# The first MoE's weights decoded in pairs of 768 columns, in place in four staging buffers

## The chip, the cores and the metric

The kernel runs on one core of one Trainium2 chip. Its time is the device time of one execution in microseconds (us); the figure for a kernel is the median over its runs. All work of the reference is done in this one launch.

## The reference

A recurrent attention with a decaying state feeds a gated MoE layer, and that feeds a second layer with SoLU and LayerNorm. 3072 tokens (4 sequences of 768) of 384 features pass through all three.

```python
# attention: r, k, v, w of shape (4, 8, 768, 48), u of (8, 48)
for t in range(S):
    cur = einsum('bhd,bhe->bhde', u[None] * kt, vt)
    y[:, :, t] = einsum('bhd,bhde->bhe', rt, state + cur)
    state = wt[:, :, :, None] * state + einsum('bhd,bhe->bhde', kt, vt)
# first MoE: w_gate, w_val (384, 1536), w_out (1536, 384)
g = x @ w_gate
x = (g / (1 + exp(-g)) * (x @ w_val)) @ w_out
# second MoE: w_in (384, 1024), w_out (1024, 384)
h = x @ w_in
solu = h * softmax(h)
out = layernorm(solu) * g_ln @ w_out
```

The weights of both MoE layers come as 64-bit floats. The kernel makes 32-bit floats of them on the chip ("decoding") and then splits each into a high part in the format fp32r and the low rest; a product is made of three matmuls (high by high, high by low, low by high).

## The kernel before

**Order.** The program first collects every operation with an engine, an assumed duration, a priority and its dependencies in a `Graph`; `emit` then plays these through a list scheduler and writes the instructions of each engine in that order. So each engine runs a fixed sequence, and a priority or an assumed duration changes where an instruction stands. A DMA is a resource of that plan like an engine; all DMAs are issued by one queue, that of SP, in the planned order, and an issue waits there until its target buffer is free.

**Blocks.** The 3072 tokens go in six groups `q` of 512 (128 of each sequence). Of the first group the first MoE runs its first six hidden tiles `m` (of 128 columns; 12 in all) on two halves of 256 tokens, one after the other, and then the other six on all 512; the groups `q` from 1 on run all 12 at 512. One such step is a unit (`moe1_unit`): nine matmuls for the gate projection (PSUM tile `ps` or `psa` from `xh`, `xl` and `hg`, `lg`; `h` and `l` for high and low), nine for the value projection (`hv`, `lv`), SiLU on ScalarE into `sg`, the product on VectorE in `sg`, its split into `mh` (copy on ScalarE) and `ml` (subtraction on VectorE), and, after the next unit's projections, nine matmuls with `ho`, `lo` that add to three PSUM banks. The attention's tiles (24, by group and sequence: `feat`, `tok`, `vv` are loaded, VectorE scans and scales) are spread between the units of the group ahead.

**Weights.** In the first group, with the first half and then with the full-width units, `weight` loads and decodes gate, value and output weights of `m`, 384 columns of 128 rows each (393 KB as 64-bit floats), at a priority 1.8 units ahead of the unit that uses them. The load goes to one of three staging tiles `st`, shifted by one byte, so that the words of the tile can be used as they lie. `decode8` then takes, for each weight:

- ScalarE copies the top bytes of the numbers to `tb` (L331 `tb<-st`, 384 bytes per row);
- VectorE's L378 and L381 rearrange bits in `tb`, 96 words each, with the start of `dc` as scratch;
- ScalarE's L384 writes `tb`, scaled, to the 384 words of `dc`;
- VectorE's L386 shifts the low word from `st` and joins it with `dc`; after it `st` is free;
- ScalarE copies `dc` to the high part (`hg`, `hv` or `ho`);
- VectorE subtracts (L328 `lg`, `lv` or `lo`); after it `dc` is free. For `m` 0 this low part is made by two matmuls into PSUM (L453, L454) and a copy on ScalarE instead.

There are two `dc` and two `tb`. Behind the first group's last unit no weight is left to decode, and the `st` tiles serve as buffers for results that go to DRAM.

**Fills.** As long as the planner finds nothing for TensorE before its time 80, it puts in matmuls of the identity (L1157). There are 81 of them in the program, 46 ahead of the first projection; each leaves two matmul records in the trace (162).

Of the kernel before, what the change touches and what calls it, by code (L numbers as in the profile page):

```python
# [38 lines left out]
NEX = 4  # L39
NFLAT = 8  # L40
# [194 lines left out]
def attn_moe_moe2_kernel(  # L235
# [88 lines left out]
    def words(src):  # L324
        return src.bitcast(U32) if wide else src
# [19 lines left out]
    def t_act(n):  # L345
        return 0.1 + n / 1200
# [15 lines left out]
    def decode(prio, st, dc, n, skey, dkey):  # L362
        if not wide:
            return st[:, 0:n], skey
        s3 = st[:, 0:2 * n].rearrange("p (n t) -> p n t", t=2)
        a = dc[:, 0:n]

        for z in range(3):
            g.add("DVE", 0.07 + (0.2 if z == 0 else 0.4) * n / DM, prio, lambda z=z: decode_op(z, s3, a), [skey], [dkey],
                  port=True)  # L370
        return a.bitcast(F32), dkey

    def decode8(prio, st, dc, t8, skey, dkey, tkey):
        tops = st.bitcast(I8)[:, 8:8 * DM + 8:8]
        b, a = t8.bitcast(I8), dc.bitcast(I32)
        n4 = DM // 4
        g.add("ACT", t_act(DM), prio, copy(b, tops), [skey], [tkey])
        g.add("DVE", 0.17, prio, lambda: DVE.tensor_scalar(out=dc[:, 0:n4], in0=t8, scalar1=0x07070707, scalar2=3,  # L378
                                                           op0=ALU.bitwise_and, op1=ALU.logical_shift_left),
              [tkey], [dkey], port=True)  # L380
        g.add("DVE", 0.17, prio, lambda: DVE.scalar_tensor_tensor(  # L381
            out=t8, in0=t8, scalar=0xC0C0C0C0, in1=dc[:, 0:n4], op0=ALU.bitwise_and, op1=ALU.bitwise_or),
              [dkey], [tkey], port=True)
        g.add("ACT", t_act(DM), prio, lambda: ACT.activation(out=a, in_=b, func=AF.Copy, scale=float(1 << 24)),  # L384
              [tkey], [dkey])
        g.add("DVE", 0.47, prio, lambda: DVE.scalar_tensor_tensor(  # L386
            out=dc, in0=st[:, 1:2 * DM:2], scalar=5, in1=dc, op0=ALU.logical_shift_right, op1=ALU.bitwise_or),
              [skey], [dkey], port=True)
        return dc.bitcast(F32), dkey
# [35 lines left out]
    def weight(w, m, prio):  # L425
        i = nst[0]
        nst[0] += 1
        st, dc = ST[i % 3], DC[i % 2]
        sk, dk = ("st", i % 3), ("dc", i % 2)
        ws, sd = words(W1[w]), st[:, 0:DM * sz]  # L430
        z = sz
        if wide:
            ws, sd, z = W1[w].bitcast(U8), st.bitcast(U8)[:, 1:8 * DM + 1], 8
        if w == "o":
            fn = dma(sd, ws[m * 128:(m + 1) * 128, :])
        else:
            fn = dma(sd.rearrange("p (k f) -> p k f", k=KD),
                     ws[:, m * 128 * z:(m + 1) * 128 * z].rearrange("(k p) f -> p k f", p=128))
        first = g.dma(0.55 * sz, prio - 10, fn, [], [sk])
        if wide:  # L440
            a, ak = decode8(prio, st, dc, TB8[i % 2], sk, dk, ("tb8", i % 2))
        else:
# [794 lines left out]
```

## Time and profile before

| | before |
|---|---|
| time, median of 3 runs | 765.27 us |
| lowest and highest | 764.41 and 766.58 us |
| span of the profiled execution | 766.4 us |
| TensorE (PE) busy | 754.6 us, 98% |
| VectorE (DVE) busy | 574.3 us, 75% |
| ScalarE (ACT) busy | 333.7 us, 44% |
| GpSimd (POOL) busy | 60.8 us, 8% |
| chain that ended last | PE 85%, DVE 6%, DMA 4%, ACT 2% |

The profile is one execution with a span of its own, 766.4 us, from its first instruction to its last; the total time of that execution is not listed apart. Busy time counts recorded instructions, overlapping ones once; the recorded time of a VectorE or ScalarE instruction is longer than the step to the next one's start, since the next starts before the last has fully drained. The chain is followed back from the last instruction, at each step to what it waited for. [...]

### The profile page before, as it was taken

The page shows a single profiled execution, that of the slowest core. Times are in us where ns is not written, and L with a number is a line of the kernel's source. Part 1 is how long each engine was busy: PE and PEld are TensorE (multiplying, and loading weights), DVE is VectorE, ACT ScalarE, POOL GpSimd, SP SyncE. Part 2 cuts the span into 40 slices and gives each one's busy share as a digit, 9 for nine tenths or more (in the row PEclk, how much of TensorE's full clock was granted, in tenths as well). Part 3 has the DMA queues.
Part 4 walks back from the last instruction along what each step waited for, and adds up shares of the span by engine and source line. Part 5 has one row for each costly group of instructions (what it writes and reads, how often), then busy time and mean ns, then how long its engine had stood idle before and what let it go on. Part 6 is the DMA issues. An engine that isn't in the chain of part 4 may idle for free.

```text
span 766.4 us, 16301 instructions
## 1 busy us (share of the span) xinstructions
PE 754.6 (98%) x6393; PEld 649.7 (85%) x6393; DVE 574.3 (75%) x1286; ACT 333.7 (44%) x747; POOL 60.8 (8%) x53
## 2 busy tenths in 40 slices
PE   8999999899999999999999999999999999999998
PEld 7899987688888888888888888888888988889998
DVE  8798998987776678667776643486788989899930
ACT  4777766353242334333334322333454442654541
POOL 0000000000000000000000000000011221623330
PEclk9999999999999999999999999999999999999999
DMA  7677575323333323323322210343331124234321
GB/s 216 178 232 234 164 233 162 113 71 89 97 104 103 98 78 94 113 78 86 96 82 88 77 40 14 117 130 114 95 124 62 54 75 114 79 100 108 92 86 47
DMA packets 60077, 83.09 MB, mean 108 GB/s; under 512 B 18272, under 2 KB 43360, under 8 KB 60000
## 3 DMA queue, kind: packets, MB, share of 16 engines
q1 hardware_dynamic: 60000, 82.05, 36.8%
q8 instruction: 50, 0.82, 0.5%
q14 instruction: 27, 0.22, 0.1%
HBM read 60.25 MB, written 10.22 MB: 92 GB/s over the span
## 4 chain that ended last, share of the span: by engine, by line
PE 85%; DVE 6%; DMA 4%; ACT 2%; SPq 1%; issue 1%; ACTq 0%; DVEq 0%
PE ps L753 15%; PE ps L754 14%; PE ps L755 14%; PE pb L1135 4%; PE pb L1136 4%; PE pb L1137 4%; PE hp L1027 4%; PE hp L1028 4%; PE hp L1029 3%; PE psa L753 3%; PE psa L755 3%; PE psa L754 3%; PE ps L1157 2%; DMA st<-w_out 2%; SPq L1120 1%; DMA st<-w_val 1%
## 5 line engine op out<-in xcount | busy, mean ns | idle before, releaser
L754 PE MATMUL ps<-ml,ho 128*128 128x512 f32 (+1 forms) x234 | 87.6, 374 | 1.2 <-DVE ml L328 1.1
L753 PE MATMUL ps<-mh,ho 128*128 128x512 f32 (+1 forms) x234 | 88.0, 376 | 0.3 <-ACT mh L331 0.3
L755 PE MATMUL ps<-mh,lo 128*128 128x512 f32 (+1 forms) x234 | 87.2, 373 | 0.0
L331 ACT ACTIVATE mh<-sg 128x512 fp32r<-128x512 f32 (+1 forms) x78 | 46.4, 596 | 87.6 <-DVE sg L328 87.1
L788 ACT ACTIVATE sg<-ps 128x512 f32<-128x512 f32 (+1 forms) x57 | 32.9, 577 | 86.9 <-PE ps L755 86.1
L328 DVE TENSOR_TENSOR ml<-sg,mh 128x512 fp32r<-128x512 f32 (+1 forms) x78 | 50.2, 645 | 26.8 <-ACT mh L331 26.6
L753 PE MATMUL ps<-xh,hg 128*128 128x512 f32 (+1 forms) x171 | 67.5, 395 | 0.3 <-DVE xl L328 0.3
L328 POOL TENSOR_TENSOR xl<-x2s,xh 128x512 fp32r<-128x512 f32 x15 | 19.7, 1330 | 601.0 <-ACT xh L331 601.0
L754 PE MATMUL ps<-xl,hg 128*128 128x512 f32 (+1 forms) x171 | 65.8, 385 | 0.0
L755 PE MATMUL ps<-xh,lg 128*128 128x512 f32 (+1 forms) x171 | 65.7, 384 | 0.0
L1135 PE MATMUL pb<-o2h,th 128*128 128x384 f32 x192 | 65.0, 338 | 0.6 <-ACT ob L331 0.6
L1137 PE MATMUL pb<-o2h,tl 128*128 128x384 f32 x192 | 64.5, 336 | 0.0
L1136 PE MATMUL pb<-o2l,th 128*128 128x384 f32 x192 | 64.5, 336 | 0.0
L328 DVE TENSOR_TENSOR sg<-sg,ps 128x512 f32<-128x512 f32 (+1 forms) x53 | 34.1, 643 | 40.0 <-PE ps L755 39.0
L753 PE MATMUL ps<-xh,hv 128*128 128x512 f32 (+1 forms) x159 | 59.6, 375 | 0.5 <-ACT sg L788 0.5
L755 PE MATMUL ps<-xh,lv 128*128 128x512 f32 (+1 forms) x159 | 59.4, 373 | 0.0
L754 PE MATMUL ps<-xl,hv 128*128 128x512 f32 (+1 forms) x159 | 59.3, 373 | 0.0
L1027 PE MATMUL hp<-i2h,xh 128*128 128x512 f32 x144 | 57.0, 396 | 0.5 <-DVE sv L1044 0.5
L1028 PE MATMUL hp<-i2l,xh 128*128 128x512 f32 x144 | 56.6, 393 | 0.0
L1029 PE MATMUL hp<-i2h,xl 128*128 128x512 f32 x144 | 56.1, 390 | 0.0
L331 ACT ACTIVATE kt<-PR 32x256 f32<-32x256 f32 (+1 forms) x128 | 46.2, 361 | 22.6 <-DVE PR L605 21.2
L754 PEld LDWEIGHTS ps<-ml,ho 128*128 128x128 f32 x234 | 44.1, 188 | 9.6 <-DVE ml L328 1.9
(184 smaller groups left out, 1901.7 us busy)
## 6 DMA issues: line engine op xcount, KB each, us to landing
tok<-tok SPq DMA_DIRECT2D x20, 576.0 KB, 3.9
feat<-feat SPq DMA_DIRECT2D x24, 448.0 KB, 4.7
xt<-tb SPq DMA_DIRECT2D x128, 64.0 KB, 2.0
feat<-feat SPq DMA_DIRECT2D x24, 231.4 KB, 2.8
vv<-vv SPq DMA_DIRECT2D x24, 192.0 KB, 4.1
st<-w_gate SPq DMA_DIRECT2D x12, 384.0 KB, 4.0
st<-w_val SPq DMA_DIRECT2D x12, 384.0 KB, 4.0
st<-w_out SPq DMA_DIRECT2D x12, 384.0 KB, 4.3
```

Of the source, the lines that this page charges most:

```text
L328: return lambda: eng.tensor_tensor(out=out, in0=in0, in1=in1, op=op)
L331: return lambda: ACT.activation(out=out, in_=in_, func=AF.Copy)
L753: PE.matmul(out=o, lhsT=wh, rhs=xhi, start=first, stop=False)
L754: PE.matmul(out=o, lhsT=wh, rhs=xlo, start=False, stop=False)
L755: PE.matmul(out=o, lhsT=wl, rhs=xhi, start=False, stop=last)
L788: lambda: ACT.activation(out=sg, in_=pg.t[:, 0:n], func=AF.Silu), [pg.key], [sk]))
L1027: PE.matmul(out=hp()[:, f], lhsT=xh_[:, k, s], rhs=R["i2h"][:, k, f], start=(k == 0), stop=False)
L1028: PE.matmul(out=hp()[:, f], lhsT=xh_[:, k, s], rhs=R["i2l"][:, k, f], start=False, stop=False)
L1029: PE.matmul(out=hp()[:, f], lhsT=xl_[:, k, s], rhs=R["i2h"][:, k, f], start=False, stop=(k == KD - 1))
L1135: PE.matmul(out=po(), lhsT=th[:, m], rhs=R["o2h"][:, m], start=(m == 0), stop=False)
L1136: PE.matmul(out=po(), lhsT=th[:, m], rhs=R["o2l"][:, m], start=False, stop=False)
L1137: PE.matmul(out=po(), lhsT=tl[:, m], rhs=R["o2h"][:, m], start=False, stop=(m == M2 - 1))
```

## The change

Weights are decoded two at a time. A pair (`duos`) is gate and value of one `m`, or the output weights of two neighbouring `m`; the order is (gate, value) of `m`, (output of `m`, output of `m`+1), (gate, value) of `m`+1, and so on for even `m`: 18 pairs in place of 36 weights. Two loads fill the halves of one staging tile, of which there are now four (`NST`), each with room for 768 numbers. Each decoding step is one instruction for both: L367 and L370 of 192 words, and L373, L375, the copy to the high part and the subtraction of 768. The tile `dc` is gone: L367 uses the even words of the staging tile as scratch, L373 writes there, L375 joins them with the odd words in place, and copy and subtraction read the odd words, 8 bytes apart. The staging tile is thus free after the subtraction. The high and low parts of a pair are one tile each, named after its first (`hg`, `lg` hold gate and value). With `m` 0 the pairs (gate, value) of 0 and (output of 0, output of 1) take the low part through PSUM, one split per half. [...] Branches for weights that are not 64-bit go.

```diff
+NST = 4
-    WH = {(w, m): w1p.tile([128, KD, 128], F32R, name=f"h{w}{m}") for m in range(M1) for w in "gvo"}
-    WL = {(w, m): w1p.tile([128, KD, 128], F32R, name=f"l{w}{m}") for m in range(M1) for w in "gvo"}
-    ST = slots(stp, "st", [128, DM * sz + 2], 3, RAW)
-    DC = slots(stp, "dc", [128, DM], 2, U32)
-    TB8 = slots(stp, "tb8", [128, DM // 4], 2, U32)
+    duos = [d for m in range(0, M1, 2) for d in ((("g", m), ("v", m)), (("o", m), ("o", m + 1)), (("g", m + 1), ("v", m + 1)))]
+    WD = {d: [w1p.tile([128, 2, KD, 128], F32R, name=f"{x}{d[0][0]}{d[0][1]}") for x in "hl"] for d in duos}
+    WH, WL = ({y: WD[d][z][:, i] for d in duos for i, y in enumerate(d)} for z in range(2))
+    sz, RAW, N2 = 2, U32, 2 * DM
+    ST = slots(stp, "st", [128, 2 * N2 + 2], NST, RAW)
+    TB8 = slots(stp, "tb8", [128, N2 // 4], 2, U32)
...
+    def decode8(prio, st, t8, skeys, okey, ekey, tkey):
+        tops = st.bitcast(I8)[:, 8:8 * N2 + 8:8]
+        odd, even = st[:, 1:2 * N2:2], st[:, 2:2 * N2 + 2:2]
+        b, n4 = t8.bitcast(I8), N2 // 4
+        g.add("ACT", t_act(N2), prio, copy(b, tops), skeys, [tkey])
+        g.add("DVE", 0.07 + n4 / 960, prio, lambda: DVE.tensor_scalar(
+            out=even[:, 0:n4], in0=t8, scalar1=0x07070707, scalar2=3, op0=ALU.bitwise_and, op1=ALU.logical_shift_left),
+              [tkey], [ekey], port=True)
+        g.add("DVE", 0.07 + n4 / 960, prio, lambda: DVE.scalar_tensor_tensor(
+            out=t8, in0=t8, scalar=0xC0C0C0C0, in1=even[:, 0:n4], op0=ALU.bitwise_and, op1=ALU.bitwise_or),
+              [ekey], [tkey], port=True)
+        g.add("ACT", t_act(N2), prio, lambda: ACT.activation(
+            out=even.bitcast(I32), in_=b, func=AF.Copy, scale=float(1 << 24)), [tkey], [ekey])
+        g.add("DVE", t_dve(N2), prio, lambda: DVE.scalar_tensor_tensor(
+            out=odd, in0=odd, scalar=5, in1=even, op0=ALU.logical_shift_right, op1=ALU.bitwise_or),
+              skeys + [ekey], [okey], port=True)
+        return odd.bitcast(F32)
...
+    def weights(duo, prio):
+        i = nst[0] % NST
...
+        for z, (w, m) in enumerate(duo):
...
+            g.dma(1.1, prio - 10, fn, [], [sk[z]])
+        a = decode8(prio, st, t8, sk, ok, ek, tk)
+        h, l = (x.rearrange("p d k f -> p (d k f)") for x in WD[duo])
+        g.add("ACT", t_act(N2), prio, copy(h, a), sk + [ok], hk)
+        if duo[0][1] >= NLO:
+            g.add("DVE", t_dve(N2), prio, tt(DVE, l, a, h.bitcast(F32), ALU.subtract), sk + [ok] + hk, lk, port=True)
         else:
+            for z in range(2):
...
+                g.add("PE", 0.9, prio, fn, sk + [ok, hk[z], "ident", "nident"], take=[ps])
+                g.add("ACT", t_act(DM), prio, lambda ps=ps, c=c: copy(l[:, c], ps.t[:, 0:DM])(), [ps.key], [lk[z]])
...
             if c0 == 0 and q == 0:
-                for w in "gvo":
-                    weight(w, m, bstart[j] + UNIT[n] * (m - m0 - 1.8))
+                for d in duos:
+                    if d[0] == ("g", m) or d[0] == ("o", m):
+                        weights(d, bstart[j] + UNIT[n] * (m - m0 - 1.8))
...
-    nc = _bacc.Bacc("TRN2", target_bir_lowering=False, num_devices=1)
+    nc = _bacc.Bacc("TRN2", target_bir_lowering=False, num_devices=1, dynamic_dma_scratch_size=1024)
```

The new instructions stand at L367 (was L378), L370 (L381), L373 (L384), L375 (L386), L441 and L442 (L453 and L454); the fills are at L1144. Of the 81 fills before, 46 stand ahead of the first projection and 35 behind it; of the 60 now, 46 and 14.

The order changes at three places. The first is SP's queue at the start, from the third weight load of before on; `st` are the staging tiles (numbers tell tiles apart), `feat`, `vv`, `tok` and `u_tok` belong to the attention. Before:

L334 DMA st_178<-w_gate 128x3x1024
L334 DMA st_179<-w_val 128x3x1024
L334 DMA st_180<-w_out 128x3072
L334 DMA feat_207<-feat 112x529
L334 DMA u_tok<-u_rep 128x384
L334 DMA feat_206<-feat 112x1024
L334 DMA vv_208<-vv 128x384
L334 DMA tok_210<-tok 128x384
L334 DMA feat_207<-feat 112x1024
L334 DMA vv_209<-vv 128x384
L334 DMA tok_211<-tok 128x384
L334 DMA st_178<-w_gate 128x3x1024
```

Now:

L334 DMA st_142<-w_gate 128x3x1024
L334 DMA st_142<-w_val 128x3x1024
L334 DMA st_143<-w_out 128x3072
L334 DMA feat_170<-feat 112x529
L334 DMA st_143<-w_out 128x3072
L334 DMA st_144<-w_gate 128x3x1024
L334 DMA st_144<-w_val 128x3x1024
L334 DMA st_145<-w_gate 128x3x1024
L334 DMA st_145<-w_val 128x3x1024
L334 DMA u_tok<-u_rep 128x384
L334 DMA feat_169<-feat 112x1024
L334 DMA vv_171<-vv 128x384
```

Three weight loads stood ahead of the eight loads of the attention that are shown, and the fourth, which waits for its tile, behind them; now eight weight loads, into all four tiles, stand ahead of all but one of these.

The second is VectorE around the second unit, with decoding steps between the attention's products (`tok`, `AM`, `e`) and the unit's (`sg`, `ml`). Before:

L386 SCALAR_TENSOR_TENSOR dc_182<-st_178,dc_182 128x384
L486 SCALAR_TENSOR_TENSOR e_212<-feat_206,pat_f 112x528
L328 TENSOR_TENSOR ml_104<-sg_100,mh_102 128x256
L328 TENSOR_TENSOR lg_145<-dc_182,hg_109 128x384
L386 SCALAR_TENSOR_TENSOR dc_181<-st_179,dc_181 128x384
L378 TENSOR_SCALAR dc_182<-tb_184 128x96
L328 TENSOR_TENSOR tok_210<-ps_80,tok_210 128x192
L381 SCALAR_TENSOR_TENSOR tb_184<-tb_184,dc_182 128x96
L328 TENSOR_TENSOR tok_210<-ps_78,tok_210 128x192
L328 TENSOR_TENSOR lv_146<-dc_181,hv_110 128x384
L386 SCALAR_TENSOR_TENSOR dc_182<-st_180,dc_182 128x384
```

Now:

L375 SCALAR_TENSOR_TENSOR st_145<-st_145 128x768
L367 TENSOR_SCALAR st_142<-tb_146 128x192
L328 TENSOR_TENSOR tok_173<-psa_85,tok_173 128x192
L328 TENSOR_TENSOR sg_101<-sg_101,psa_84 128x256
L370 SCALAR_TENSOR_TENSOR tb_146<-tb_146,st_142 128x192
L328 TENSOR_TENSOR lg_113<-st_145,hg_112 128x768
L328 TENSOR_TENSOR ml_105<-sg_101,mh_103 128x256
L375 SCALAR_TENSOR_TENSOR st_142<-st_142 128x768
L328 TENSOR_TENSOR tok_173<-ps_80,tok_173 128x192
L367 TENSOR_SCALAR st_143<-tb_147 128x192
L328 TENSOR_TENSOR AM_155<-ps_78,mask_sb 128x512
L328 TENSOR_TENSOR lo_115<-st_142,ho_114 128x768
```

Decoding is now one instruction of 768 columns where two of 384 stood, and other instructions still stand between the steps of one pair.

The third is TensorE ahead of the first projection, where the low parts of `m` 0 are made through PSUM (L453 and L454, then L441 and L442) and `xh` is the attention's result that the projection reads. Before:

L453 MATMUL ps_79<-dc_181,ident 128x384
L454 MATMUL ps_79<-hg_106,nident 128x384
L742 MATMUL ps_78<-xh_96,nident 128x128 x3
L731 MATMUL psa_84<-ident,tok_211 128x128 x3
L453 MATMUL psa_85<-dc_182,ident 128x384
L454 MATMUL psa_85<-hv_107,nident 128x384
L1157 MATMUL ps_80<-ident 128x128
L742 MATMUL psa_84<-xh_96,nident 128x128 x3
L1157 MATMUL ps_80<-ident 128x128 x4
L579 MATMUL ps_80<-ident,feat_206 128x112 x4
L581 MATMUL ps_80<-u_sb,PR_193 128x2 x4
L532 MATMUL ps_79<-feat_206 64x64 x16
```

Now:

L441 MATMUL psa_84<-st_142,ident 128x384
L442 MATMUL psa_84<-hg_106,nident 128x384
L730 MATMUL ps_79<-xh_96,nident 128x128 x3
L441 MATMUL psa_85<-st_142,ident 128x384
L442 MATMUL psa_85<-hg_106,nident 128x384
L441 MATMUL ps_80<-st_143,ident 128x384
L442 MATMUL ps_80<-ho_108,nident 128x384
L441 MATMUL ps_78<-st_143,ident 128x384
L442 MATMUL ps_78<-ho_108,nident 128x384
L520 MATMUL ps_79<-feat_169 64x64 x16
L1144 MATMUL psa_84<-ident 128x128 x2
L567 MATMUL psa_84<-ident,feat_169 128x112 x4
```

The split of a second output weight (`ho`) has come in. Of an attention tile's products, which stood ahead of the first projection with all their 16 matmuls of `vv` and `kt` (further rows of before), now only those of `feat` do.

## Rows read from the trace of the kernel before

**Rows 1.** Busy time by stretch: stretch, length, each engine, granted clock, DMA share, GB/s.

```profile
34.00:80.00 46.00, 45.67 (x621) 43.69 (x621) 41.81 (x122) 35.43 (x92) 0.00 (x0) 1.00 0.71 215
80.00:150.00 70.00, 66.70 (x726) 56.00 (x725) 65.07 (x168) 44.22 (x102) 0.00 (x0) 0.99 0.57 168
160.00:430.00 270.00, 270.00 (x2705) 222.96 (x2696) 195.38 (x416) 97.27 (x214) 0.00 (x0) 1.00 0.32 94
```

**Rows 2.** The same view, instructions of line 1157 (fills) alone, 34 to 80 us.

```profile
34.00:80.00 46.00, 11.06 (x74) 9.04 (x73) 1.00 0.71 215
```

**Rows 3.** Chain of waits, 108 to 130 us: start, us, what.

```profile
112.80 6.67 DMA st<-w_out
...
119.55 0.55 ACT tb L331
...
120.13 0.21 DVE dc L378
...
123.06 5.62 DMA feat<-feat
```

**Rows 4.** Waits of VectorE, 39 to 148 us: total, times, longest.

```profile
DVE ml L328 <- ACT mh L331: 2.4, 3, 1.2
DVE dc L378 <- ACT tb L331: 2.0, 4, 0.8
DVE feat L328 <- DMA feat<-feat: 0.9, 1, 0.9
```

**Rows 5.** Who waited for the staging tiles st: us, times.

```profile
  ACT tb L331: 10.0, 15
```

**Rows 6.** Waits of the SP queue, 34 to 130 us.

```profile
SPq L334 <- DVE dc L386: 25.2, 14, 4.2
```

**Rows 7.** Timeline of VectorE: start, us, line, operation, out<-in, shapes.

```profile
102.54 0.66 DVE L328 TENSOR_TENSOR ml<-sg,mh 128x512 fp32r<-128x512 f32 x1
103.13 0.55 DVE L328 TENSOR_TENSOR lo<-dc,ho 128x384 fp32r<-128x384 f32 x1
103.60 0.55 DVE L328 TENSOR_TENSOR xl<-psa,xh 128x384 fp32r<-128x384 f32 x1
104.06 0.34 DVE L328 TENSOR_TENSOR RO<-ps,RE 112x192 f32<-112x192 f32 x1
104.33 0.24 DVE L381 SCALAR_TENSOR_TENSOR tb<-tb,dc 128x96 uint32<-128x96 uint32 x1
104.49 0.35 DVE L328 TENSOR_TENSOR RO<-RO,zt 112x192 f32<-112x192 f32 x1
104.76 0.20 DVE L378 TENSOR_SCALAR dc<-tb 128x96 uint32<-128x96 uint32 x1
104.88 0.35 DVE L328 TENSOR_TENSOR TS<-ps,RO 112x192 f32<-112x192 f32 x1
105.16 0.56 DVE L386 SCALAR_TENSOR_TENSOR dc<-st,dc 128x384 uint32<-128x384 uint32 x1
105.64 0.25 DVE L381 SCALAR_TENSOR_TENSOR tb<-tb,dc 128x96 uint32<-128x96 uint32 x1
```

**Rows 8.** Timeline of ScalarE, around 55 us.

```profile
55.36 0.51 ACT L331 ACTIVATE hg<-dc 128x384 fp32r<-128x384 f32 x1
55.78 0.40 ACT L331 ACTIVATE mh<-sg 128x256 fp32r<-128x256 f32 x1
```

**Rows 9.** Timeline of TensorE, 148 to 153 us; idle time before in brackets.

```profile
148.59 0.50 PE L754 MATMUL ps<-ml,ho 128*128 128x512 f32 x1 [1.07 <-DVE ml L328]
...
149.46 0.63 PE L754 MATMUL ps<-xl,hg 128*128 128x512 f32 x1
...
152.80 0.39 PE L753 MATMUL ps<-xh,hv 128*128 128x512 f32 x1
153.03 0.39 PE L754 MATMUL ps<-xl,hv 128*128 128x512 f32 x1
```

**Rows 10.** Chain of waits near 25 us: one split through PSUM.

```profile
25.32 0.65 PE ps L453 x2
```

More of the change, by code (lines that the diff above doesn't have):

```diff
@@ L324, in words @@
     def words(src):
-        return src.bitcast(U32) if wide else src
+        return src.bitcast(U32)
     def tt(eng, out, in0, in1, op):
@@ L360, in decode_op @@
                                      op0=ALU.logical_shift_right, op1=ALU.bitwise_or)
[L362 to L389, printed above, removed]
@@ L423, in attn_moe_moe2_kernel @@
     st_nodes = []
-    def weight(w, m, prio):
-        i = nst[0]
+    def weights(duo, prio):
+        i = nst[0] % NST
+        t8, tk = TB8[nst[0] % 2], ("tb8", nst[0] % 2)
         nst[0] += 1
[L428 to L435, printed above, removed]
-        else:
[L437 to L442, printed above, removed]
-            a, ak = decode(prio, st, dc, DM, sk, dk)
-        h, l = (x[w, m].rearrange("p k f -> p (k f)") for x in (WH, WL))
-        if m >= NLO:
-            split(prio, h, l, a, DM, [ak], ("wh", w, m), ("wl", w, m))
-        else:
-            g.add("ACT", t_act(DM), prio, copy(h, a), [ak], [("wh", w, m)])
-            ps = g.bank(ALL)
-            def fn():
-                o = ps.t[:, 0:DM]
-                PE.matmul(out=o, lhsT=ident, rhs=a, start=True, stop=False)
-                PE.matmul(out=o, lhsT=nident, rhs=h, start=False, stop=True)
-            g.add("PE", 0.9, prio, fn, [ak, ("wh", w, m), "ident", "nident"], take=[ps])
-            g.add("ACT", t_act(DM), prio, lambda: copy(l, ps.t[:, 0:DM])(), [ps.key], [("wl", w, m)])
@@ new lines, in weights @@
+        st, sk = ST[i], [("st", i, z) for z in range(2)]
+        ok, ek = ("so", i), ("se", i)
+        first = len(g.opts)
+        for z, (w, m) in enumerate(duo):
+            ws, sd = W1[w].bitcast(U8), st.bitcast(U8)[:, 8 * DM * z + 1:8 * DM * (z + 1) + 1]
+            if w == "o":
+                fn = dma(sd, ws[m * 128:(m + 1) * 128, :])
+            else:
+                fn = dma(sd.rearrange("p (k f) -> p k f", k=KD),
+                         ws[:, m * 1024:(m + 1) * 1024].rearrange("(k p) f -> p k f", p=128))
+            g.dma(1.1, prio - 10, fn, [], [sk[z]])
@@ L810, in later @@
                     if late:
[L811 removed]
+                        xs, xk = ST[k].bitcast(F32), [("st", k, 0), ("st", k, 1)]
                     else:
                         xs, xk = sg_slot() if q == 0 or k < 2 else (None, "x2s0")
+                        xk = [xk]
                     def spill(k=k, xs=xs):
@@ L953, in step @@
         def step(z, i=i, cn=cn, raw=raw):
-            if wide:
-                decode_op(z, R["st"][i][:, 0:2 * cn].rearrange("p (n t) -> p n t", t=2), raw())
-            elif z == 0:
-                DVE.tensor_copy(out=raw().bitcast(F32), in_=R["st"][i][:, 0:cn])
+            decode_op(z, R["st"][i][:, 0:2 * cn].rearrange("p (n t) -> p n t", t=2), raw())
         def w2v(nm, k=k, c0=c0, cn=cn):
```

15 lines of the change are left out of this document (9 added, 6 removed).

## Prediction

> **What bounds the kernel now.** The page names TensorE busy for 98% of the span, an average over stages with different limits. I read it in four steps. First the busy times by stretch. From 160 to 430 us TensorE is fed by itself: VectorE needs 195.38 of 270 us. From 34 to 150 us, the only stretch with decoding of the first MoE's weights, VectorE is busy 41.81 of 46 and 65.07 of 70 us [rows 1], 92% together, and 74 of the records that make TensorE look full in the first of these are matmuls of the identity that keep it running, 11.06 us of them [rows 2]. So a gain can come from this stretch alone, TensorE's useful work there being fixed.
>
> Second, the chain of waits. Around 113 us it leaves TensorE: a load into a staging buffer takes 6.67 us, ScalarE's first decoding step waits for it, VectorE waits for that step, and VectorE's step then frees the buffer for the next load, behind which the attention's feat load stands, 5.62 us more [rows 3]. Third, who waits: VectorE waits 2.4 us for mh, 2.0 us for decoding step 1 on ScalarE and 0.9 us for feat, the three that matter of eight rows with 7.6 us in all [rows 4]; ScalarE waits 10.0 us in 15 places for the staging loads [rows 5]; SP's queue stands 25.2 us in 14 places before a load whose buffer the last decoding step has not yet freed [rows 6]. Fourth, TensorE at the end of the stretch: it waits 1.07 us for ml from VectorE [rows 9]. VectorE is what comes last, and staging is why it is not at 100%.
>
> **The change, part by part.** *Less issue time on VectorE.* One instruction's price is the step to the next start, not its recorded time: 384 columns step 0.47 us (103.13 to 103.60) and 0.48 (105.16 to 105.64), 512 step 0.59 (102.54 to 103.13), 96 step 0.16 (L381, 104.33 to 104.49) or 0.12 (L378, 104.76 to 104.88), 192 step 0.27 (104.06 to 104.33) [rows 7]. From 384 to 512 that is 0.12 us for 128 columns, so 768 columns step 0.47 + 3 x 0.12 = 0.83 to, by 0.59 + 2 x 0.14 with the mean slope from 192, 0.87; I take 0.87. Two weights cost 2 x (0.12 + 0.16 + 0.48 + 0.47) = 2.46 us now; a pair costs 0.27 for L370, 2 x 0.87 for L375 and the subtraction, and for L367 between 0.17 (it keeps the pace of L378) and 0.27 (it falls to L381's): 2.18 to 2.28. Sixteen pairs save 16 x 0.18 to 0.28 = 2.9 to 4.5 us. The first two pairs have no subtraction on VectorE, the second output weight's now among them: 3 x 0.76 + 1.23 = 3.51 against 2 x 1.31 to 1.41, 0.7 to 0.9 us. Together 3.6 to 5.4; I take 4.5.
>
> *Words that are no longer contiguous.* L373 now writes, L375 reads and writes, and the copies read 4-byte words 8 bytes apart. The old last step already reads its word so, and steps as the contiguous subtraction does, 0.48 against 0.47 [rows 7]: no price for reading. No row shows such a write. Bounds: nothing (as reading), or half pace, 0.80 us for each L375, 14.4 for 18. I take nothing, since the nearest row is the read of the same words. [...]
>
> *Staging.* Four buffers of two weights replace three of one: SP issues eight weight loads before the first release where it issued three, as the order shows. A load then has three pairs' work to land in. VectorE's waits that go: most of that for mh, where ScalarE's queue stood for a load ahead of it (I count 1.7 of the 2.4), the 2.0 for step 1, and the 0.9 for feat, whose issue stood behind a weight load [rows 3, 4]: 4.6 us. The lower bound is 2.0 (step 1 alone), the upper all 7.6. ScalarE's 10.0 us go too and are worth nothing by themselves: it is busy 35.43 of 46 us, then 44.22 of 70 [rows 1]. A buffer is now held through the subtraction, since the decoded word stays in it; with four that is hidden by the three others, and if a pair took longer than three pairs' work the wait would be back.
>
> *New waits.* Each pair passes VectorE to ScalarE and back three times, with wider steps: ScalarE's 384-column copy steps 0.42 (55.36 to 55.78) [rows 8], and at VectorE's slope one of 768 columns 0.36 more. If VectorE found nothing else each time, 18 x 0.36 = 6.5 us at the extreme for one such wait per pair; nothing if other work always stands between. The order puts two to nine of VectorE's other instructions between the steps that pass through ScalarE, so I take 1.0, near the lower end.
>
> *The start.* The first unit needs two weights decoded instead of one, but nothing is moved behind an attention load, and the order puts the first projection ahead of the second attention tile's update. Bounds: 2.1 us later (a pair's chain has five wide steps, 0.36 to 0.40 us longer each, and two small ones, 0.1 longer) and as much earlier, which no row splits. I take 1.0 earlier, since the order moved the projection forward. *TensorE* gets one more split through PSUM, 0.65 us [rows 10], on the path where TensorE is full later: it costs 0.65. Counted in the order, 14 of 35 fills behind the first projection remain; they stand where TensorE would wait anyway and give nothing back by themselves.
>
> [...]
>
> **Sum.** 4.5 + 4.6 + 1.0 - 1.0 - 0.65 = 8.4 us. Until unit 18 TensorE follows VectorE's ml, so time gained there counts in full, and behind it TensorE is full at a fixed amount of work. The profiled execution has a span of 766.4 us, 1.1 above the median of the three runs, 765.27, and 0.2 below the highest, 766.58; what lies around the span is small. 766.4 - 8.4 = 758.0, and from the median 765.3 - 8.4 = 756.9; I say **757.0 us**.
>
> **Rivals.** *VectorE's issue time alone.* If the staging waits only move, because VectorE at 92% would wait elsewhere [rows 1], the gain is 4.5 - 0.65 = 3.9, so 761.4. For it: eight waits are spread over ScalarE, DMA and the mh copies [rows 4]; against it: the largest three share one cause [rows 3].
>
> *Later pairs.* Wider steps give the first result later. New waits at 6.5 instead of 1.0 and the start 2.1 later instead of 1.0 earlier take 8.6: the time is 765.5, unchanged. For it: each step's wait is 0.36 us longer where nothing stands between; against it: something nearly always does, by the order. [...]
>
> *Strided writes, the slower side.* If L375 writes at half pace, VectorE pays 14.4 us more in the stretch where it is last, and the sum turns to -6.0: 771.3. It decides from 8.4 / 18 = 0.47 us for each L375. For it: no row has such a write with three strided operands; against it: the strided read is free [rows 7].
>
> [...]
>
> *The loads set the pace.* If the transfers, not the buffers, were short, prefetching would change nothing beyond issue time; the DMA engines are busy 0.71 and 0.57 of the stretch [rows 1], so they are not full, and this falls in with the first rival.
>
> **How the numbers follow.** Forecast (gain 4.6 to 14): 0.62. Issue time alone, the loads among it: 0.15. Cold TensorE: 0.05. Later pairs: 0.10. Strided writes: 0.08. A measurement of this kernel can tell about 0.3%, 2.3 us, from no change: faster means under 763.0, slower over 767.6. Faster: 0.62 + 0.14 + 0.03 + 0.01 = 0.80; the same: 0.01 + 0.01 + 0.08 = 0.10; slower: 0.01 + 0.01 + 0.08 = 0.10. The range: with every term at its good end 5.4 + 7.6 + 2.0 - 0.65 = 14.4, so 751 from the median, 750.5 with a little of the clock; at the other end it takes in issue time alone and reaches into the later pairs, 764.5; what is left out is the slower side, most of the later pairs and the best ends, 0.19.
>
> **What would show it.** Right: in the profile after, ScalarE's wait for staging loads from 10.0 to under 3 us; SP's wait for the last decoding step far under 25; L375 and the subtraction with steps near 0.87 and recorded times near 0.95 us; VectorE busy over 94% from 34 us to the end of decoding and decoding over some 8 us sooner; fills about 24 records between 34 and 80 us; the same work from 160 us on, only sooner. Wrong: L375 over 1.3 us; new VectorE waits for L373 or the copies of more than 4 us in all; a granted clock under 1 in more places than one; or the same end of decoding with the gain given back before unit 18.

## The result

The changed kernel takes 758.83 us in the median (757.92 to 759.95) beside 765.69 us for the kernel before (764.41 to 766.58): a ratio of 0.990 with a 95% interval of 0.988 to 0.992, 6.9 us faster. The forecast was 757.0 us, in a range of 750.5 to 764.5. The profiled execution has a span of 757.7 us, 8.7 under that of before; single executions of one kernel lie up to 5 us apart (763.45 to 768.75 for the kernel before in one round of the experiments), so I size effects by the medians and use the profiles to find places.

The windows of the changed kernel, in the stretches and columns of [rows 1], and behind them the fills alone, as in [rows 2] (the granted clock is a share of TensorE's full speed, L12 is line 12 of a kernel, `out<-in` are tile names without their numbers, `x` counts records):

```profile
34.00:80.00 46.00, 45.30 (x535) 43.32 (x535) 43.04 (x93) 39.33 (x82) 0.00 (x0) 1.00 0.79 246
80.00:150.00 70.00, 69.59 (x949) 57.97 (x949) 66.97 (x150) 39.41 (x82) 0.00 (x0) 1.00 0.44 134
160.00:430.00 270.00, 270.00 (x2676) 222.95 (x2675) 191.55 (x407) 98.06 (x218) 0.00 (x0) 1.00 0.32 91
```

```profile
34.00:80.00 46.00, 4.27 (x24) 3.13 (x24) 1.00 0.79 246
```

VectorE is busy 43.04 of the first 46 us (41.81 before) and TensorE 69.59 of the 70 behind them (66.70 before), with 24 records of fills in place of 74. From 160 us on TensorE is full as before.

VectorE's waits from 39 to 148 us (total, times, longest), for [rows 4]; the line that answers to [rows 5]; and that of SP's queue, for [rows 6]:

```profile
DVE st L367 <- ACT tb L331: 1.2, 1, 1.2
...
DVE lg L328 <- ACT hg L331: 0.5, 2, 0.3
DVE ml L328 <- ACT mh L331: 0.5, 2, 0.2
```

```profile
  ACT tb L331: 3.0, 4
```

```profile
SPq L334 <- DVE lg L328: 10.9, 4, 3.4
```

ScalarE's wait for staging loads fell from 10.0 to 3.0 us and VectorE's for `mh` from 2.4 to 0.5. SP's queue waits 10.9 us for the subtraction (`lg`) now, which holds the tile; the last decoding step cost it 25.2 us before. The last subtraction of a weight starts at 124.0 us, before the change at 139.6.

The wide steps on VectorE (start, recorded us; a step is the difference of two starts):

```profile
55.63 0.95 DVE L375 SCALAR_TENSOR_TENSOR st<-st 128x768 uint32<-128x768 uint32 x1
56.50 0.41 DVE L328 TENSOR_TENSOR sg<-sg,ps 128x256 f32<-128x256 f32 x1
56.84 0.26 DVE L367 TENSOR_SCALAR st<-tb 128x192 uint32<-128x192 uint32 x1
57.00 0.42 DVE L328 TENSOR_TENSOR feat<-feat,e 112x256 f32<-112x256 f32 x1
57.34 0.35 DVE L370 SCALAR_TENSOR_TENSOR tb<-tb,st 128x192 uint32<-128x192 uint32 x1
57.61 0.42 DVE L328 TENSOR_TENSOR feat<-feat 112x256 f32<-112x256 f32 x1
...
64.14 0.96 DVE L328 TENSOR_TENSOR lg<-st,hg 128x768 fp32r<-128x768 f32 x1
65.02 0.95 DVE L375 SCALAR_TENSOR_TENSOR st<-st 128x768 uint32<-128x768 uint32 x1
```

L375 steps 0.87 us, L367 0.16 and L370 0.27, and the subtraction ends its step after 0.88 (64.14 to 65.02). Over the first 160 us of the trace, where the next instruction follows without a wait, the median steps are 0.869, 0.169, 0.269 and 0.865 us, beside 0.468, 0.119, 0.167 and 0.468 for a narrow one. So a pair costs 2.17 us in place of 2.44, and VectorE saves 16 x 0.27 + 0.9 = 5.2 us: the forecast's 3.6 to 5.4 at its upper end. L375, which writes words 8 bytes apart, steps as long as the subtraction, which writes them next to one another (0.869 and 0.865 us): in this trace such writes cost nothing.

Two further places matter below. In unit 15 (units count from 0; 17 is the last of the first group) VectorE's `ml` starts at 120.76 and TensorE's first matmul with it at 129.70:

```profile
120.76 0.67 DVE L328 TENSOR_TENSOR ml<-sg,mh 128x512 fp32r<-128x512 f32 x1
```

```profile
129.70 0.39 PE L742 MATMUL ps<-ml,ho 128*128 128x512 f32 x1
```

And at unit 17 TensorE's wait for `ml` is 0.41 us, where it was 1.07 [rows 9], with a granted clock of 1.00 from 145 to 150 us behind it:

```profile
140.60 0.40 PE L741 MATMUL ps<-mh,ho 128*128 128x512 f32 x1
141.41 0.50 PE L742 MATMUL ps<-ml,ho 128*128 128x512 f32 x1 [0.41 <-DVE ml L328]
141.75 0.39 PE L743 MATMUL ps<-mh,lo 128*128 128x512 f32 x1
```

```profile
145.00:150.00 5.00, 5.00 (x142) 4.20 (x141) 4.30 (x11) 3.38 (x8) 0.00 (x0) 1.00 0.16 59
```

### The profile page after: what moved, and what is told of

Same layout as the page of the kernel before. It is cut to its first block, busy times and chain, and to the rows that moved or that the text cites. A ratio compares the mean times of both kernels' runs of the same rounds, so it can differ in the third digit from the quotient of the medians.

```text
span 757.7 us, 16058 instructions
## 1 busy us (share of the span) xinstructions
PE 748.4 (99%) x6354; PEld 643.8 (85%) x6354; DVE 569.4 (75%) x1215; ACT 328.5 (43%) x694; POOL 60.6 (8%) x53
## 4 chain that ended last, share of the span: by engine, by line
PE 89%; DVE 4%; ACT 2%; DMA 2%; SPq 1%; issue 1%; ACTq 0%; DVEq 0%
PE ps L741 15%; PE ps L742 15%; PE ps L743 15%; PE pb L1122 4%; PE pb L1124 4%; PE pb L1123 4%; PE hp L1014 4%; PE hp L1015 4%; PE hp L1016 4%; PE psa L741 4%; PE psa L743 3%; PE psa L742 3%; PE ps L1144 2%; DMA st<-w_out 2%; PE ps L626 1%; SPq L1107 1%
## 5 line engine op out<-in xcount | busy, mean ns | idle before, releaser
L741 PE MATMUL ps<-xh,hg 128*128 128x512 f32 (+1 forms) x330 | 126.2, 382 | 0.6 <-ACT sg L776 0.6
L743 PE MATMUL ps<-xh,lg 128*128 128x512 f32 (+1 forms) x330 | 124.4, 377 | 0.0
L742 PE MATMUL ps<-xl,hg 128*128 128x512 f32 (+1 forms) x330 | 124.4, 377 | 0.0
L742 PE MATMUL ps<-ml,ho 128*128 128x512 f32 (+1 forms) x234 | 87.4, 374 | 0.5 <-DVE ml L328 0.4
L741 PEld LDWEIGHTS ps<-xh,hg 128*128 128x128 f32 x330 | 62.1, 188 | 12.5 <-ACT sg L776 0.8
L743 PEld LDWEIGHTS ps<-xh,lg 128*128 128x128 f32 x330 | 62.1, 188 | 11.5
L742 PEld LDWEIGHTS ps<-xl,hg 128*128 128x128 f32 x330 | 62.1, 188 | 11.0
L328 DVE TENSOR_TENSOR ml<-sg,mh 128x512 fp32r<-128x512 f32 (+1 forms) x78 | 50.5, 647 | 26.6 <-ACT mh L331 26.6
L328 DVE TENSOR_TENSOR sg<-sg,ps 128x512 f32<-128x512 f32 (+1 forms) x59 | 38.3, 650 | 41.2 <-PE ps L743 40.5
L328 POOL TENSOR_TENSOR xl<-x2s,xh 128x512 fp32r<-128x512 f32 x15 | 19.6, 1326 | 592.2 <-DVE ex L1031 558.7
L776 ACT ACTIVATE sg<-ps 128x512 f32<-128x512 f32 (+1 forms) x51 | 29.1, 571 | 83.3 <-PE ps L743 83.0
L741 PE MATMUL psa<-xh,hg 128*128 128x512 f32 (+1 forms) x138 | 51.8, 375 | 0.0
```

The costliest lines, as they stand in the source:

```text
L328: return lambda: eng.tensor_tensor(out=out, in0=in0, in1=in1, op=op)
L741: PE.matmul(out=o, lhsT=wh, rhs=xhi, start=first, stop=False)
L742: PE.matmul(out=o, lhsT=wh, rhs=xlo, start=False, stop=False)
L743: PE.matmul(out=o, lhsT=wl, rhs=xhi, start=False, stop=last)
L776: lambda: ACT.activation(out=sg, in_=pg.t[:, 0:n], func=AF.Silu), [pg.key], [sk]))
```

## The experiments

Each is an edit of the kernel before or of the changed one, timed beside the kernel before on the same chip, whose medians there were 765.0 to 765.9 us. The first theory was that of the forecast: VectorE comes last, so its saved issue time counts in full, and the staging tiles take waits away on top. The rivals were that the staging alone, or the issue time alone, made the gain.

### half_width: narrow steps, the staging as it is

```diff
-        g.add("ACT", t_act(N2), prio, copy(b, tops), skeys, [tkey])
+        for z in range(2):
+            decode_half(prio, tops[...], odd[...], even[...], t8[...], skeys[z:z + 1], okey + (z,), ekey + (z,), tkey + (z,))
```

(with each further step, copy and subtraction as an operation of its own for each half)

> Staging as in the changed kernel (four tiles of two weights, loads and places alike, words still 8 bytes apart), but each decoding step, copy and subtraction is two instructions of 384 columns again. Theory (VectorE's issue time counts in full beside the staging): VectorE gets 16 x 0.27 + 0.9 = 5.2 us back by the steps of the two traces, so about 764.0 against 758.8. Rival, staging alone made the gain: 758.8, unchanged. Rival, later pairs cost time that narrow steps win back: under 758.

Measured: 763.9 us (762.74 to 765.59), ratio to before 0.998 (0.997 to 1.000). That is the first theory's number, 5.1 us above the changed kernel. But the edit also gives the planner twice the decoding operations, and so another order on every engine.

### before_st8: deep staging, single weights

```diff
-    ST = slots(stp, "st", [128, DM * sz + 2], 3, RAW)
+    ST = slots(stp, "st", [128, DM * sz + 2], 8, RAW)
-        st, dc = ST[i % 3], DC[i % 2]
+        st, dc = ST[i % 8], DC[i % 2]
```

(and `dynamic_dma_scratch_size=1024`, as in the changed kernel)

> The kernel before with eight staging tiles of one weight in place of three (same numbers ahead as four of two), the smaller scratch area, nothing else; instructions stay 384 wide and the two dc stay. Theory: the waits for staging go and the width stays, so 1.7 (what the measured 6.9 us leave beside 5.2 of issue time) to 4.6 us (the forecast's term) below 765.7: 761 to 764. Rival, issue time alone: 765.7. Rival, staging alone: 758.8.

Measured: 762.55 us, ratio 0.996 (0.995 to 0.998): 2.9 us gained of 6.9 by deeper staging, as the theory had it. The planner makes an order of its own for eight tiles, so the 2.9 us are the staging's together with that order's; no run deepens the staging in the order of the kernel before. In its trace ScalarE's first decoding step, which waited 10.0 us for staging tiles before [rows 5], is no longer among those who wait for one.

### two_tiles and three_tiles: pairs through fewer tiles

```diff
-        i = nst[0] % NST
+        i = nst[0] % 2      # two_tiles; 3 in three_tiles
```

> The changed kernel with its pairs going through two of the four staging tiles only (the memory stays as it is). Width is kept, loads come late again. Theory: the staging's share is lost, 1.7 to 4.6 us, so 760.5 to 763.4, and SP's queue waits for the subtraction again. Rival, issue time alone: 758.8. Rival, staging alone: back to about 765.7 or above.

> The changed kernel with its pairs going through three of the four staging tiles (memory as it is). Two tiles cost 11.9 us. If a tile is short only while one is loaded, one decoded and one subtracted, three are enough: 759 to 760. If the fourth buys as the third did: about 764.

Measured: 770.68 us with two (ratio 1.007, 1.005 to 1.009), 761.3 with three (0.995, 0.993 to 0.996): 11.9 and 2.5 us above the changed kernel. The theory's number for two, 760.5 to 763.4, was too low; the rival of staging alone, "about 765.7 or above", takes in the number, but before_st8, 3.7 us above the changed kernel, speaks against that rival. None priced the hold: a tile now keeps its pair through the subtraction. That the hold is the reason is argued, not shown: SP's queue waits 14.2 us for the subtraction of `lg` with two tiles and 10.9 with four, but no run frees a tile sooner. With three tiles the time lies between the two that were expected, 759 to 760 and 764. ScalarE's wait for the loads, two tiles and then three:

```profile
  ACT tb L331: 10.6, 8
```

```profile
  ACT tb L331: 7.9, 6
```

With two tiles there is room for four weights against three before, and still it is 5.3 us slower than the kernel before beside it (765.4). The third tile buys 9.4 us, the fourth 2.5.

### l370_twice and l370_five: more issue time in the same order

```diff
-        g.add("DVE", 0.07 + n4 / 960, prio, lambda: DVE.scalar_tensor_tensor(
-            out=t8, in0=t8, scalar=0xC0C0C0C0, in1=even[:, 0:n4], op0=ALU.bitwise_and, op1=ALU.bitwise_or),
+        g.add("DVE", 0.07 + n4 / 960, prio, lambda: [DVE.scalar_tensor_tensor(
+            out=t8, in0=t8, scalar=0xC0C0C0C0, in1=even[:, 0:n4], op0=ALU.bitwise_and, op1=ALU.bitwise_or) for _ in range(2)],
```

(`range(5)` in the second)

> The changed kernel with L370 issued twice in a row in each of the 18 pairs (the second changes nothing in the data), in the same order: 18 x 0.27 = 4.8 us more on VectorE. Theory: VectorE comes last in the stretch and the time is paid nearly in full, 763.0 to 763.7. Rival, staging alone, VectorE has room: under 760.

> L370 five times in each pair in the changed kernel's order: 4 x 18 x 0.27 = 19.4 us more on VectorE. If some 4 us are hidden by idle time and the rest is paid: about 774. If VectorE never comes last: under 763. If every us is paid from the second on, as the first theory had it: 777 to 778.

Measured: 759.83 us (759.12 to 760.53) with 4.8 us more on VectorE, of which 1.0 is paid by the medians and 2 by the ratios to before (0.993 and 0.990); 777.46 us with 19.4 more, of which 18.6 is paid. The first theory falls with the first number: in the changed kernel's order VectorE has idle time that takes up more than half of 5 us. Beyond that each us is paid, and more than once: the 14.5 us between the two kernels cost 17.6. Two windows of l370_five, in the columns of [rows 1]:

```profile
34.00:60.00 26.00, 23.52 (x326) 22.19 (x325) 25.45 (x60) 19.91 (x47) 0.00 (x0) 0.93 0.61 187
...
80.00:110.00 30.00, 26.54 (x259) 24.31 (x259) 29.43 (x69) 17.93 (x33) 0.00 (x0) 0.94 0.49 157
```

There TensorE waits, busy 23.52 of 26 us and 26.54 of 30, and the granted clock reads 0.93 and 0.94.

### halves_same_order and all_halves_same_order: the width alone

```diff
-            out=odd, in0=odd, scalar=5, in1=even, op0=ALU.logical_shift_right, op1=ALU.bitwise_or),
+            out=odd[:, c], in0=odd[:, c], scalar=5, in1=even[:, c], op0=ALU.logical_shift_right, op1=ALU.bitwise_or) for c in cut(N2)],
```

(likewise for L367, L370 and the subtraction; in the second also for ScalarE's three steps; durations told to the planner unchanged)

> The changed kernel in its own order on every engine; only VectorE's decoding steps (L367, L370, L375, the subtraction) are each issued as two halves, one behind the other, in the place of the one: 5.2 us of issue time back on VectorE, nothing else. Theory (new: in the order of the changed kernel VectorE has idle time that hides most of an addition; the 5 us of half_width came with another order): 759.5 to 760.5. Rival, issue time is paid: 763 to 764.

> As the one before, and ScalarE's three wide steps of each pair as two halves too: 18 x 0.17 = 3.1 us more on ScalarE by the steps of the traces (768 columns against two of 384: 0.80 against 0.91, 0.78 against 0.83, 0.80 against 0.83). All instructions are then as narrow as in half_width, in the order of the changed kernel. Theory (order): 760 to 761. Rival, issue time of both engines: 763 to 764 as half_width.

Measured: 758.78 us (758.35 to 760.44) and 758.85 (758.04 to 759.82), no different from 758.83. The narrow instructions are there, two behind one another in one place, 1.02 us for what one does in 0.95:

```profile
57.52 1.02 DVE L378 SCALAR_TENSOR_TENSOR st<-st 128x384 uint32<-128x384 uint32 x2
...
60.90 1.02 DVE L328 TENSOR_TENSOR lo<-st,ho 128x384 fp32r<-128x384 f32 x2
```

and VectorE is busier for it. The sums of the four windows from 34 to 130 us, first of the changed kernel, then of halves_same_order:

```profile
sum 96.00, PE 95.30 PEld 85.64 DVE 90.84 ACT 69.83 POOL 0.00; mean PE 23.83 PEld 21.41 DVE 22.71 ACT 17.46 POOL 0.00
```

```profile
sum 96.00, PE 95.25 PEld 86.33 DVE 94.75 ACT 69.89 POOL 0.00; mean PE 23.81 PEld 21.58 DVE 23.69 ACT 17.47 POOL 0.00
```

VectorE stood idle 5.2 of 96 us in the changed kernel, and 1.25 with the halves: in this order the issue time that the wide steps save is time in which VectorE has nothing else to do. TensorE is busy 95.3 of the 96 us in both, fills among them, and the timelines show that VectorE does not pace it: from its first matmul with `ml` of unit 9 to that of unit 16 TensorE takes 56.66 us in the changed kernel, and the same 56.66 in halves_same_order, in all_halves_same_order and in l370_twice (63.6 in l370_five). No run puts the wide instructions into the order of the kernel before; what the width would be worth there stays open. And all_halves_same_order and half_width run the same narrow instructions, 5.1 us apart; only the order, and which half waits for what, differ.

### order_of_narrow: the order alone

```diff
-        g.add("DVE", t_dve(N2), prio, lambda: DVE.scalar_tensor_tensor(
+        g.add("DVE", 2 * 0.47, prio, lambda: DVE.scalar_tensor_tensor(
```

(likewise for every step of a pair: the planner is told the duration of two narrow ones)

> The changed kernel's wide instructions; only the planner is told that each step lasts as long as two narrow ones, so the order moves toward that of half_width while no instruction changes. Theory (the order places VectorE's attention work so that it is behind at units 16 to 18): 761 to 764. Rival, issue time alone: 758.8.

Measured: 760.9 us (760.11 to 763.41), ratio 0.994 (0.992 to 0.996): 2.1 us above the changed kernel with not one instruction changed. It is just under the theory's 761 to 764; the rival, 758.8, lies outside what was measured. But its trace doesn't show the theory's place. By the table under scan_behind_ml TensorE takes 21.0 us from unit 16 to unit 19 and 21.3 in the changed kernel, so nothing is lost there, and in unit 17 it doesn't wait for `ml` at all. What the trace shows to differ lies ahead of these units: 140 records of fills in place of 120, 22.9 us in place of 20.4, with 0.5 us less of idle time.

### before_st6_dc4: the changed kernel's memory for single weights

```diff
-    DC = slots(stp, "dc", [128, DM], 2, U32)
+    DC = slots(stp, "dc", [128, DM], 4, U32)
```

(with six `st` and four `tb`)

> The kernel before with six staging tiles of one weight, four dc and four tb in place of three, two and two: the memory of the changed kernel, single weights of 384 columns, contiguous dc. Theory (what before_st8 still lacked at the start, 4.4 us of it in fills up to 80 us, is buffers for decoded words: in the changed kernel eight weights can stand between L367 and the subtraction, in before_st8 two): 759 to 760.5. Rival, the pairs' width gives the rest: 762.5 as before_st8. Rival, any order that the planner makes of single weights is as bad at units 16 to 18: 762 to 764.

Measured: 762.52 us, ratio 0.996 (0.995 to 0.997), as before_st8. Buffers for decoded words are not what was missing, at six staging tiles. The number fits both rivals, 762.5 and 762 to 764. Its last subtraction starts at 130.3 us, 3 us sooner than in before_st8, and nothing comes of it.

### scan_behind_ml: one place in the order

To see where the order costs, here is the start of TensorE's first matmul with `ml` of a unit, read from each timeline, and in the last two rows TensorE's fills up to 150 us and its idle time from 34 to 150 us (all in us):

| unit | before | before_st8 | half_width | scan_behind_ml | order_of_narrow | all_halves_same_order | changed |
|---|---|---|---|---|---|---|---|
| 9 | 92.4 | 88.5 | 80.7 | 82.6 | 83.2 | 80.5 | 82.1 |
| 16 | 144.2 | 140.4 | 138.4 | 140.2 | 140.7 | 137.2 | 138.8 |
| 17 | 148.6 | 144.0 | 143.1 | 143.7 | 147.2 | 139.8 | 141.4 |
| 19 | 168.9 | 162.7 | 163.5 | 163.6 | 161.7 | 158.5 | 160.1 |
| 24 | 203.9 | 197.7 | 198.5 | 198.6 | 196.7 | 193.5 | 195.1 |
| fills | 26.7 | 25.9 | 22.1 | 22.1 | 22.9 | 19.8 | 20.4 |
| idle | 3.6 | 0.9 | 1.9 | 2.5 | 0.6 | 0.9 | 1.1 |

Profiles of one and the same order lie up to 2.7 us apart in such rows (unit 9: 80.5 here, 83.2 in halves_same_order), so what lies between two rows of a column says more than two columns in a row.

Up to unit 16 half_width is level with the changed kernel (138.4 and 138.8); at unit 19 it is 3.4 us behind, and stays so: from unit 16 to 19 it takes 25.1 us in place of 21.3. (In order_of_narrow the matmuls of unit 17 stand behind more of the next unit's projections, so that row doesn't compare.) VectorE at unit 17 of half_width, then TensorE and its window, in the columns of [rows 1]:

```profile
140.12 0.69 DVE L328 TENSOR_TENSOR sg<-sg,ps 128x512 f32<-128x512 f32 x1
140.72 0.62 DVE L328 TENSOR_TENSOR tok<-psa,tok 128x192 f32<-128x192 f32 x2
141.26 1.25 DVE L484 TENSOR_TENSOR_SCAN e<-feat,pat_f 112x528 f32<-112x528 f32 x1
142.42 0.67 DVE L328 TENSOR_TENSOR ml<-sg,mh 128x512 fp32r<-128x512 f32 x1
...
143.17 0.49 DVE L328 TENSOR_TENSOR xl<-ps,xh 128x384 fp32r<-128x384 f32 x1
```

```profile
141.13 0.70 PE L729 MATMUL ps<-ident,tok 128*128 128x128 f32 x3 [0.78 <-DVE tok L328]
...
143.14 0.50 PE L752 MATMUL ps<-ml,ho 128*128 128x512 f32 x1 [1.07 <-DVE ml L328]
...
145.09 0.63 PE L752 MATMUL ps<-xl,hg 128*128 128x512 f32 x1
145.51 0.63 PE L753 MATMUL ps<-xh,lg 128*128 128x512 f32 x1
...
147.59 0.40 PE L752 MATMUL ps<-xl,hg 128*128 128x512 f32 x1
147.82 0.40 PE L753 MATMUL ps<-xh,lg 128*128 128x512 f32 x1
```

```profile
145.00:150.00 5.00, 5.00 (x18) 3.97 (x17) 4.08 (x9) 2.66 (x8) 0.00 (x0) 0.75 0.31 104
```

Between `sg` and `ml` of this unit the order puts the next attention tile's scan, 1.16 us. TensorE waits 1.07 us for `ml`, and behind it steps 0.42 us (145.09 to 145.51), where it steps 0.23 a little later (147.59 to 147.82); the granted clock reads 0.75 from 145 to 150 us. The same scan stands there in the kernel before, in before_st8 and in before_st6_dc4; in the changed kernel three short products of the attention do. The last experiment exchanges these two instructions of half_width:

```diff
+        x = calls.pop(at[scan])     # calls: the planned order
+        calls.insert(at[ml], x)     # ml: that of unit 17
```

> half_width with two neighbouring instructions of VectorE exchanged and nothing else: the attention's scan (e from feat, a step of 1.16 us), which its order puts between sg and ml of unit 17, goes right behind that ml. In the profile of half_width TensorE waits 1.07 us for this ml, and behind it 8 matmuls step 0.43 instead of 0.23 us, the granted clock of 145 to 150 us being 0.75: some 2.6 us in all. The same scan stands there in the kernel before and in before_st8 and before_st6_dc4, and not in the changed kernel. Theory (what narrow steps lose at units 16 to 18 is this place in the order): 761 to 762. Rival, VectorE has too much to do there and the wait only moves: 763.9.

Measured: 762.57 us (761.99 to 762.86), 1.3 under half_width where 1.9 to 2.9 were expected; the intervals of the two ratios (0.997 to 1.000, and 0.995 to 0.998) overlap a little. The timeline of TensorE shows the half that failed:

```profile
142.59 0.70 PE L740 MATMUL ps<-ident,tok 128*128 128x128 f32 x3 [0.41 <-DVE tok L338]
...
143.71 0.50 PE L763 MATMUL ps<-ml,ho 128*128 128x512 f32 x1 [0.18 <-DVE ml L338]
...
145.58 0.49 PE L763 MATMUL ps<-xl,hg 128*128 128x512 f32 x1 [0.91 <-DVE xl L338]
145.91 0.39 PE L764 MATMUL ps<-xh,lg 128*128 128x512 f32 x1
146.14 0.40 PE L762 MATMUL ps<-xh,hg 128*128 128x512 f32 x1
```

The wait for `ml` is 0.18 us and the matmuls step 0.23 again (145.91 to 146.14), but now `xl`, which stood behind `ml` and stands behind the scan, comes late: a new wait of 0.91. So the wait itself moved, as the rival said, and what was won is the pace behind it, with a granted clock of 1.00 from 145 to 150 us in place of 0.75. The single executions point the same way: the mean granted clock reads 0.998 in nine of the twelve of half_width (median 764.1 us) and 1.000 in the other three (763.0), and 1.000 in four of the five of scan_behind_ml (762.6). One exchange does not make the changed kernel's order. Of the 3.7 us that are left, the table's last rows show 1.7 more of fills and 1.4 more of idle time than in the changed kernel; which part of the order makes them stays open.

### feat_first: the loads that crowd the start

```diff
+            if nst[0] == 4:
+                fn = lambda fn=fn: held_loads.append(fn)     # issued behind feat of the third tile
             g.dma(1.1, prio - 10, fn, [], [sk[z]])
```

> The changed kernel with one move on SP's queue alone: the two loads of the fourth pair are issued behind the third attention tile's 448 KB feat load (which they stand ahead of now), all other engines in the order as it is. In the changed kernel's profile VectorE waits 2.28 us for that feat near 26 us, behind 2 MB of weight loads issued from 15 to 18 us; before the change such a wait was 0.3. Theory (loading ahead crowds the feat load and costs the start): that wait falls under 1 us and the time to 757 to 758. Rival, the start is not on the path, or the fourth pair then comes late: 758.8 or more.

Measured: 758.51 us (758.16 to 759.02), not different. The wait is real and goes; VectorE in the changed kernel, and then in feat_first:

```profile
25.45 0.35 DVE L370 SCALAR_TENSOR_TENSOR tb<-tb,st 128x192 uint32<-128x192 uint32 x1
28.09 0.69 DVE L328 TENSOR_TENSOR PR<-feat 112x512 f32<-112x512 f32 x1 [2.28 <-DMA feat<-feat]
```

```profile
25.89 0.35 DVE L370 SCALAR_TENSOR_TENSOR tb<-tb,st 128x192 uint32<-128x192 uint32 x1
26.55 0.69 DVE L328 TENSOR_TENSOR PR<-feat 112x512 f32<-112x512 f32 x1 [0.30 <-DMA feat<-feat]
...
30.51 0.96 DVE L375 SCALAR_TENSOR_TENSOR st<-st 128x768 uint32<-128x768 uint32 x1 [0.64 <-ACT st L373]
```

But VectorE then waits 0.64 us for ScalarE's step of a pair, and TensorE's first matmul with `ml` starts no sooner (42.1 us, 41.7 in the changed kernel). The start was not held by this load.

## Why the prediction came out right

**The total was right, one of its two large terms was not.** The 8.4 us of the sum were 6.9, but they are not made as the sum had it. Nearly all that the forecast named as signs is there: steps of 0.87 us, 24 records of fills, 3.0 us of ScalarE's wait for loads (under 3 was said), VectorE 95% busy from 34 to 150 us (43.04 and 66.97 of 116); decoding ends 15.6 us sooner where 8 were said. These signs tell that the work and the waits have the forecast sizes. They did not tell what these are worth. A term that was worth nothing and one that was left out nearly cancelled; that the total fits is in part luck.

**Issue time, 4.5 us.** The size on the engine was right (5.2 by the steps of the trace after, with L367 at its lower bound), its worth was not: in the changed kernel's order two narrow instructions in each place cost nothing (758.78), and 4.8 us more cost 1 to 2. The step that failed is in the sum: that until unit 18 TensorE follows VectorE's `ml`, so that time gained counts in full. From unit 12 to 16 the matmuls start 6 to 9 us behind `ml`, as shown for unit 15, and in the trace of before it was 4 to 8: 127.1 and 135.0 for unit 15. At units 2 to 9 they start 1 to 3 us behind it, but there too nothing is paid: from unit 0 to unit 9 TensorE takes 40.5 us in the changed kernel, 39.8 with the halves and 40.6 with L370 twice. VectorE's busy share of 92% [rows 1] was read as an engine that is short of time; the 5.2 us that it is idle in the changed kernel are just as large as the term. The rival of issue time alone falls with this too: its number, 761.4, lies 2.6 us above what was measured, and its mechanism is not there.

**Staging, 4.6 us.** Measured as 2.9 with single weights (interval 1.8 to 3.9), between the bounds of 2.0 and 7.6. That four tiles hide the hold through the subtraction fits three tiles, which cost 2.5. What fewer tiles cost was not priced: two of them lose more than the whole change brings.

**Order, not in the sum at all.** By elimination about 4 us of the 6.9 are neither staging (before_st8, 762.55) nor width (halves_same_order) nor buffers (before_st6_dc4); this is an estimate, since before_st8 and before_st6_dc4 each have an order of their own. That order can be worth as much is shown: the same narrow instructions lie 5.1 us apart in two orders, and durations told to the planner alone move 2.1 us (order_of_narrow). The last rows of the table tell the two parts from one another. From before to before_st8 TensorE's idle time falls from 3.6 to 0.9 us and the fills hardly; from there to the changed kernel the fills fall from 25.9 to 20.4 us and the idle time doesn't. Fills stand where the plan had nothing for TensorE, so this part comes with the plan; whether a fill costs time or stands where TensorE would wait, no run separates. In the working the order was used to count what stands between two steps and which fills are left, and taken as given otherwise. The wait of 1.07 us for `ml` at unit 17 [rows 9] was seen, but not the scan in front of `ml`. Behind it eight matmuls of before step 0.42 us (149.46 to 152.80, 3.34 us), where the next steps 0.23, and the granted clock reads 0.93 from 145 to 150 us and 0.73 from 150 to 155. That pace is gone from the profile of the changed kernel (1.00 in both windows), but little of it is in the medians: of 49 executions of the kernel before beside the experiments, 15 read a mean granted clock of 0.998, as the profiled one does (median 766.4 us), and 34 read 1.000 (765.0).

**The clock.** A cold TensorE has 0.05 of the chances, and the low end of the range takes in a little of the clock; no run shows either as a term of its own. What the runs show: with 24 records of fills in place of 74 from 34 to 80 us, and 120 in place of 162 up to 150 us, the granted clock of the changed kernel reads 1.00 in all three windows, beside 1.00, 0.99 and 1.00 before [rows 1].

**The start, 1.0 us earlier.** Its reason looked one way only: it asked whether a weight load had moved behind an attention load, and not the reverse. The third tile's `feat` now lands behind five weight loads, a wait of 2.28 us. It cost nothing (feat_first). Runs with one and the same order place the first matmul with `ml` between 41.1 and 43.4 us, so a term of 1 us at the start can't be settled by one profile.

**New waits, 1.0 us.** VectorE's waits for L367 and `lg` are 1.2 and 0.5 us, 1.7 together: near the size that was taken.

**Strided writes.** L375 at 0.869 us lies where the rows of reads had put it; the slower side would have begun 0.47 us higher.

**Later pairs.** This rival took 6.5 us of new waits and a time of 765.5; 1.7 us of such waits and 758.83 were measured. Broken up in place, the steps of a pair won or lost no time (halves_same_order, 758.78); broken up with the planner free to move the halves, 5.1 us were lost (half_width, 763.9). No run here shows a gain by it.

## What to carry to other kernels

In a program whose order a list scheduler makes, a change of widths, buffers or durations is also a change of order, and the order can be worth more than the instructions (5.1 us against none here): run the new instructions in the old order, or the old instructions in the new one, before an effect is put down to them. An engine that is 92 to 95% busy and comes last at some units may still have idle time as large as the saving (5.2 of 96 us here); look unit by unit how long its result lies before it is used. And count the buffers when each is held through one step more: the same change with two tiles is slower than no change (770.68 us beside 765.4).

## What was not expected of the hardware

L367 takes 0.05 us for 96 further columns (0.119 to 0.169) where L370 takes 0.10 (0.167 to 0.269), and keeps that pace with a write 8 bytes apart. On TensorE a wait of 1.07 us, with one of 0.78 ahead of it, was followed in half_width by matmuls that step 0.42 us in place of 0.23, the granted clock of 145 to 150 us reading 0.75; in scan_behind_ml waits of 0.41, 0.18 and 0.91 us at the same place were not (0.23 us from 145.91 on, granted clock 1.00). The program alone doesn't settle it: of twelve executions of half_width nine read a mean granted clock of 0.998 and three 1.000, and before_st8, with the same scan in front of `ml` and 0.8 us of waiting there, reads 0.999 or 1.000 in all seven. What separates them was not tried.
